# A four-step FFT filter and a low-rank token mixer on one core: last FFT stage and low-rank product in one matmul over 96 rows

## The chip, the cores and the metric

One core of one Trainium2 chip. The metric is the device time of the whole kernel in microseconds (us). Executions of one kernel mostly lie within about 1% of their median; now and then one falls into a slower state, in which the TensorE clock in the trace's records is lower throughout. Only fast executions are compared here. The core's own span in a profile is some 2 us shorter than the device time. In the profile lines PE stands for TensorE's matmuls, PEld for its weight loads, DVE for VectorE, ACT for ScalarE, POOL for GpSimd and SPq for SyncE's queue, which issues DMAs. The **pitch** of matmuls is the time from the start of one to the start of the next.

## The reference, cut to what matters

```python
X = np.fft.rfft(x, axis=1)                 # x: (8, 3136, 256)
y = np.fft.irfft(X * F, n=3136, axis=1)    # F: a complex filter per frequency and channel
h = y.T @ U @ V                            # along the sequence, rank 32
u = y + h.T
out = u + relu(u @ w_ch1) @ w_ch2          # 256 -> 1024 -> 256
```

The kernel writes 3136 as 64 x 49 and runs the FFT as matmuls: a first stage (`pf`, 64 points), a middle stage per frequency k1 (`pz` forward, multiply by the filter, `pe` back, 49 points), and a last stage (`pu`, 64 points back). The eight batches go through in five **units**: one batch each in units 0 and 1, two each in units 2, 3 and 4. While one unit's tokens go through the last stage and the two layers of the MLP (`phh`, `pc`), the next unit's first and middle stages are dealt in between.

## The kernel before: the parts that matter

The spectrum of a unit goes to DRAM (`ct2`) and is read back once, into tiles of 128 rows: 64 rows for one half of the residues r, 64 for the other. These tiles serve twice. The low-rank pass makes H = (U-hat)^T E from them:

```python
def low_rank(u):
    for rp in range(24):
        s, j, g = rp // 12, rp % 12, rp % 4
        nc.tensor.matmul(ph[32 * g:32 * g + 32, 0:bd],
                         ut2[:, rp * RANK:(rp + 1) * RANK],
                         u.e2[j // cj][:, s, j % cj, :], ...)
    ...                                            # one more for r = 48
    nc.scalar.copy(u.h1, ph[:, 0:bd])              # 4 partial sums of 32 rows
```

and the last stage reads them again, and adds H V by a second set of matmuls:

```python
def stage4(gr):                                    # a group is 512 tokens
    for dh in range(2):
        for i in range(4):                         # 8 matmuls of 128 columns in all
            nc.tensor.matmul(pu[:, dh, i * 128:(i + 1) * 128],
                             e2[:, y, j % cj + jj, d0:d0 + 128], s2, ...)
        for b in range(nb):                        # 4 of 256 columns in all
            nc.tensor.matmul(po[:, b], u.h1[:, d0:d0 + 128], vv[...], ...)
    nc.vector.tensor_copy(gr.ut, pu)
```

The plan deals the work in steps of about 1 us: the spectrum's loads 24 or 25 steps before a large unit's first group, the low-rank pass 6 steps before it. The order of each engine's instructions is fixed when the kernel is built.

## Time and profile before

| kernel before | |
|---|---|
| time, median | 634.8 us (632.4 to 640.6), 3 runs |
| span of the profiled run | 630.4 us |
| PE busy | 90% |
| bytes moved by DMA | 98.3 MB |

Two lines of the page, the granted clock in 40 slices of the span (9 is 90% of full speed or more) and the memory traffic:

```profile
PEclk9975569999999999999999999999999999999999
...
HBM read 59.88 MB, written 51.38 MB: 177 GB/s over the span
```

After the first unit's start every slice is at 9: the clock records are at full from 88 us to the last matmuls, and TensorE stands still for at most 3.2 us at a time. As **markers** I use the start of VectorE's cast to `ut` of each unit's first group: 81.5, 176.0, 259.2, 388.9 and 515.2 us in the kernel before. The two stretches in which the next unit's work is dealt most densely (columns: length; busy time and count of PE, PEld, DVE, ACT, POOL; clock; DMA share; GB/s):

```profile
81.50:176.00 94.50, 84.04 (x598) 56.63 (x597) 52.08 (x67) 50.59 (x102) 27.37 (x46) 0.96 0.94 222
176.00:259.20 83.20, 81.70 (x548) 51.80 (x547) 53.76 (x53) 49.82 (x91) 10.06 (x16) 1.00 0.72 187
```

The queue of SyncE at the end of unit 2's middle stage: the last spectrum store, output stores, and the first loads of that spectrum, which wait for the store to land.

```profile
227.31 0.32 SPq L360 DMA_DIRECT2D ct_2<-esb  x1
...
230.45 2.02 SPq L420 DMA_DIRECT2D e_2415<-ct_2  x2
```

3.1 us pass from the issue of the store to the loads. The pass's first matmul is at 248.4 in that trace, 18 us after the first load was issued; the pass's last tile, whose loads were issued from 236.9, was used at 256.2 after a wait of 0.2 us.

### The profile page before, as it was taken

To read this page: it belongs to the slowest core of one execution; us is meant where nothing else is said; L and a number is where in the kernel's file an instruction comes from. 1 tells how busy PE (TensorE), PEld (TensorE's weight loads), DVE (VectorE), ACT (ScalarE), POOL (GpSimd) and SP (SyncE) were. 2 spreads that over 40 slices of the span, in tenths; PEclk is the share of its full clock that TensorE was granted. 3 is DMA by queue.
4 is the path that set the end of the run, shared out by engine and by line. 5 is a ranking of instruction groups with operands and counts; after the bars stand their busy time and mean duration, and the time that the engine had idled before them with its cause. 6 is when DMAs were issued, how large, how long until landed. Compare 5 with 4: busy or idle time off the path is not lost.

```text
span 630.4 us, 10659 instructions
## 1 busy us (share of the span) xinstructions
PE 567.5 (90%) x4161; PEld 404.9 (64%) x4161; DVE 323.1 (51%) x376; ACT 332.1 (53%) x618; POOL 83.2 (13%) x136
## 2 busy tenths in 40 slices
PE   3178289799899999999999999999999999999995
PEld 0166146556556656667677677776777777777774
DVE  5165125676478853337777643476777223233231
ACT  0033046466366656464666665556565555555552
POOL 4230524314100113120001110100000000000000
PEclk9975569999999999999999999999999999999999
DMA  9797689999965579775437685826242753123033
GB/s 164 187 229 185 134 187 220 236 239 218 211 211 154 130 182 285 199 175 144 130 103 174 145 222 190 216 79 185 78 123 75 156 156 101 37 65 101 1 101 109
DMA packets 51993, 98.28 MB, mean 156 GB/s; under 512 B 7386, under 2 KB 29816, under 8 KB 51746
## 3 DMA queue, kind: packets, MB, share of 16 engines
q1 hardware_dynamic: 38742, 69.23, 40.0%
q0 software_dynamic: 11232, 27.20, 21.4%
q10 hardware_dynamic: 1968, 1.17, 0.7%
q8 instruction: 32, 0.52, 0.4%
q14 instruction: 19, 0.16, 0.1%
HBM read 59.88 MB, written 51.38 MB: 177 GB/s over the span
## 4 chain that ended last, share of the span: by engine, by line
PE 76%; DMA 18%; ACT 2%; SPq 1%; issue 1%; DVE 1%; POOL 0%; ACTq 0%; POOLq 0%
PE phh L497 24%; PE pc L541 23%; PE pe L347 8%; PE pz L379 5%; PE pu L482 3%; PE pu L488 3%; PE pc L513 3%; DMA ct_1<-esb 3%; DMA e_2424<-ct_2 3%; PE pf L285 2%; DMA a_342<-ct_0 2%; SPq L420 1%; DMA a_848<-ct_1 1%; DMA a_217<-ct_0 1%; DMA e_540<-ct_0 1%; DMA tf_77<-tf 1%
## 5 line engine op out<-in xcount | busy, mean ns | idle before, releaser
L497 PE MATMUL phh<-ut,w1sb 128*128 128x512 f16 (+2 forms) x848 | 245.8, 369 | 1.8 <-DVE ut L491 1.3
L394 DVE TENSOR_TENSOR uv<-pz,fab 98x1024 f16<-98x1024 f32 (+1 forms) x132 | 141.8, 1087 | 47.6 <-PE pz L379 46.1
L551 DVE COPY och<-pc 128x512 f32<-128x512 f32 x96 | 66.2, 690 | 148.4 <-PE pc L513 131.7
L358 ACT CAST esb<-pe 98x512 f16<-98x512 f32 (+1 forms) x160 | 79.9, 501 | 97.0 <-PE pe L347 78.4
L497 PEld LDWEIGHTS <-w1sb 128*128 128x128 f16 x848 | 105.9, 145 | 31.6 <-issue 8.9
L347 PE MATMUL pe<-uv,g_80 98*98 98x512 f16 (+1 forms) x330 | 90.3, 361 | 1.2 <-DMA g_80<-g 1.2
L491 DVE CAST ut<-pu 128x1024 f16<-128x1024 f32 x48 | 58.7, 1224 | 36.9 <-PE pu L488 36.0
L347 PEld LDWEIGHTS <-g_80 98*98 98x98 f16 x330 | 44.5, 138 | 18.3 <-issue 4.7
L513 PE MATMUL pc<-idn,ut 128*128 128x128 f16 x394 | 55.0, 219 | 0.0
L156 POOL DMA_DIRECT2D x<-in_x_dram x48 | 26.2, 558 | 181.4 <-PE pf L285 169.8
L379 PEld LDWEIGHTS <-tf_77 98*98 98x98 f16 x165 | 22.6, 137 | 32.8 <-issue 21.5
L513 PEld LDWEIGHTS <-ut 128*128 128x128 f16 x394 | 38.5, 98 | 6.8 <-issue 0.8
L290 DVE CAST asb<-pf 128x1024 f16<-128x1024 f32 x21 | 25.6, 1221 | 19.6 <-PE pf L285 18.8
L387 DVE TENSOR_TENSOR uv<-pz,fab 98x512 f16<-98x512 f32 x33 | 22.6, 691 | 12.5 <-PE pz L384 12.1
L285 PE MATMUL pf<-x,wf_64 128*128 128x512 f16 x84 | 25.7, 379 | 0.1
L288 ACT CAST asb<-pf 128x1024 f16<-128x1024 f32 x21 | 21.3, 1012 | 4.7 <-PE pf L285 4.2
L379 PE MATMUL pz<-a_168,tf_77 98*98 98x256 f16 x4 | 1.6, 406 | 14.7 <-DMA a_168<-ct_0 14.3
L433 PEld LDWEIGHTS <-ut_96 128*32 128x32 f16 x120 | 3.1, 101 | 16.0 <-DMA e_537<-ct_0 8.8
L305 POOL DMA_DIRECT2D ct_4<-asb x12 | 8.3, 700 | 36.2 <-ACT asb L288 36.2
L305 POOL DMA_DIRECT2D ct_2<-asb x12 | 8.5, 713 | 29.5 <-ACT esb L358 25.8
L358 ACT ACT_TABLE_LOAD x1 | 1.3, 1283 | 20.2 <-DMA ct_0<-asb 20.2
L285 PEld LDWEIGHTS <-wf_64 128*128 128x128 f16 x84 | 7.4, 98 | 4.3 <-issue 1.6
(1477 smaller groups left out, 1122.3 us busy)
## 6 DMA issues: line engine op xcount, KB each, us to landing
out_dram<-och SPq DMA_DIRECT2D x96, 192.0 KB
x<-in_x_dram POOLq DMA_DIRECT2D x48, 256.0 KB, 7.3
out_dram<-och SPq DMA_DIRECT2D x16, 384.0 KB
ct_2<-asb POOLq DMA_DIRECT2D x12, 256.0 KB, 6.5
ct_3<-asb POOLq DMA_DIRECT2D x12, 256.0 KB, 6.3
ct_4<-asb POOLq DMA_DIRECT2D x12, 256.0 KB, 5.6
ct_2<-esb SPq DMA_DIRECT2D x15, 196.0 KB
ct_3<-esb SPq DMA_DIRECT2D x15, 196.0 KB
```

Of the source, the lines that this page charges most:

```text
L156: nc.gpsimd.dma_start(t[64 * p:64 * p + 64], dram(x.tensor, (u.b[0] * SEQ + 8 * c) * DM + st * p, [[NR * DM, 64], [1, 8 * DM]]))
L285: nc.tensor.matmul(pf[:, i, :], wf1, u.x[c][:, r:r + 2, :], start=True, stop=True)
L290: nc.vector.tensor_copy(dst, pf)
L347: nc.tensor.matmul(pe[0:98, 0:bd], g3[:, (2 * k + l) * 98:(2 * k + l + 1) * 98], uv[:, l * bd:(l + 1) * bd], start=(k != 32 and l == 0), s ...
L358: nc.scalar.copy(st["esb"][:, i, :], pe[0:98, 0:bd])
L379: nc.tensor.matmul(pz[0:98, 0:bd], wz, a2[c][:, i, :], start=True, stop=True)
L394: nc.vector.tensor_mul(uv.rearrange("p (f b d) -> p f b d", f=2, b=nb), zin, fin)
L491: nc.vector.tensor_copy(gr.ut, pu)
L497: nc.tensor.matmul(ph[:, 0:n], w1v[:, dh, :, t], gr.ut[:, dh, 0:n], start=(dh == 0), stop=(dh == 1))
L513: nc.tensor.matmul(o[:, dh * 128:dh * 128 + 128], gr.ut[:, dh, t0:t0 + n], idn, start=False, stop=(dh == 1), skip_group_check=True)
L541: nc.tensor.matmul(o, gr.h[tt][:, i * 128:(i + 1) * 128], w2sb[:, tt * DM:(tt + 1) * DM], start=(tt == 0), stop=False, skip_group_check=True)
L551: nc.vector.tensor_copy(dst, gr.pc.rearrange("p (b j d) -> p b j d", b=u.nb, j=u.jc))
```

## The change

Intent: TensorE is the bound, so give it fewer columns. H is copied into rows 64 to 95 of the spectrum's own tile, and the moving operand is the table of the last stage over the matching columns of V. One matmul over 96 rows then does both products: 16 of 64 columns a group in place of 8 of 128 and 4 of 256. The price: the tiles hold 64 spectrum rows, so the low-rank pass, which wants 128, loads the spectrum a second time into a ring of three tiles of its own; H must be summed over its four partial sums and put on rows 64 to 95 by a matmul (`pk`); and H must be copied into every tile before the last stage can start. Apart from this the two real frequencies, k1 = 0 and 32, share one slot of the middle stage.

The diff, cut to its core:

```diff
-NK = 33
+NK = 32
 ...                                  # tables and filter rows for 32 slots
+    eb = [cst.tile([128, 8 * 512], F16, name=f"eb{i}") for i in range(3)]
+    def put_h(u, t, n):
+        nc.vector.tensor_copy(t[64:96, 0:n * bd]..., <u.h1 rows 64:96, repeated n times>)
+    def load_tiles():                 # as tiles come free
+            nc.sync.dma_start(t[0:64, 0:8 * bd], dram(u.ct2, 8 * c * bd, ...))
+            if u.h1 is not None and c < 3:
+                put_h(u, t, 8)
     def low_rank(u):
+        for c in range(3):
+            load(c)                   # ring of 3 tiles "eh", 128 rows
+        load_tiles()
+        yield
+        for c in range(nt):           # 3 pieces in a small unit, 6 in a large one
+            for i in range(nr): nc.tensor.matmul(ph[...], ut2[...], eh[c][:, i, :], ...)
+            if c + 3 < nt: load(c + 3)
+            if c + 1 < nt: yield
+        nc.scalar.copy(hp, ph[:, 0:bd])
+        nc.tensor.matmul(pk[0:96, 0:bd], kr, hp, start=True, stop=True)
+        nc.scalar.copy(u.h1[64:96, :], pk[64:96, 0:bd])
+        for c in sorted(u.e2): put_h(u, u.e2[c], 8)
+        put_h(u, u.e2l, 1)
     def stage4(gr):
+                nc.tensor.matmul(pu[:, dh, 64 * i:64 * i + 64], e2[0:96, d0:d0 + 128],
+                                 sv[0:96, 64 * r:64 * r + 64], ...)
-    deal(mids[2], 34, 44, S[2] - 25)  # loads at S - 24, the pass at S - 6
+    deal(mids[2], 33, 44, S[2] - 27)
+    deal_rank(units[2], S[2] - 26, S[2] - 7)   # loads at S - 26, bursts from S - 17 to S - 7
```

## The prediction

> **What bounds the kernel now.** I read the page first, then the table of stretches, then the timeline of TensorE in the steady part, at a boundary between two units (a unit is one or two batches) and round a low-rank pass.
>
> ```profile
> PE 567.5 (90%) x4161; PEld 404.9 (64%) x4161; DVE 323.1 (51%) x376; ACT 332.1 (53%) x618; POOL 83.2 (13%) x136
> PE 76%; DMA 18%; ACT 2%; SPq 1%; issue 1%; DVE 1%; POOL 0%; ACTq 0%; POOLq 0%
> ```
>
> The chain that ended last is 76% PE. The stretches (columns: length, then PE, PEld, DVE, ACT and POOL busy, granted clock, DMA share, GB/s) show where it is not:
>
> ```profile
> 30.00:66.00 36.00, 29.61 (x135) 23.85 (x133) 23.21 (x37) 12.16 (x34) 9.77 (x14) 0.65 0.85 192
> 82.80:178.00 95.20, 85.30 (x603) 57.32 (x603) 52.86 (x67) 51.17 (x103) 27.17 (x45) 0.97 0.93 224
> 260.00:414.00 154.00, 151.43 (x1140) 109.59 (x1138) 89.13 (x89) 94.61 (x168) 17.72 (x28) 1.00 0.63 164
> 414.00:520.00 106.00, 106.00 (x822) 77.42 (x820) 61.60 (x62) 64.06 (x119) 0.00 (x0) 1.00 0.48 127
> ```
>
> Up to 82.8 us the first unit waits on DMA. From 82.8 to 178 us DMA is 93% busy, and the chain runs partly through it. After 178 us PE is the bound. Busy PE overcounts, so I summed start-to-start pitches instead. The timeline has 0.216 us for 512 columns and 0.109 for 256; for 128 and 64 columns it shows:
>
> ```profile
> 404.57 0.60 PE L497 MATMUL phh<-ut,w1sb 128*128 128x512 f16 x2
> 405.01 0.39 PE L482 MATMUL pu<-s_78,e_4122 128*128 128x128 f16 x4
> 405.23 0.38 PE L488 MATMUL pu<-vsb,h_4428 128*128 128x256 f16 x2
> 405.45 0.39 PE L482 MATMUL pu<-s_78,e_4122 128*128 128x128 f16 x4
> 405.68 0.38 PE L488 MATMUL pu<-vsb,h_4428 128*128 128x256 f16 x2
> 405.89 0.27 PE L541 MATMUL pc<-w2sb,h_4512 128*128 128x256 f16 x1
> ...
> 280.16 0.19 PE L469 MATMUL pu<-s_78,e2l_97 128*128 128x64 f16 x1
> 280.19 0.19 PE L471 MATMUL pu<-vsb,h_2673 128*128 128x64 f16 x1
> 280.22 0.19 PE L469 MATMUL pu<-s_78,e2l_97 128*128 128x64 f16 x1
> ```
>
> Four matmuls of 128 columns take 0.22 us, 55 ns each; those of 64 take 29 ns each, every one behind a new stationary load of 128 columns. One group's last stage is 0.88 us (405.01 to 405.89). Summing pitches over all matmuls gives 523.6 us; of the elapsed time PE is short by 21 us in 82.8 to 178, by 8 in 178 to 260 and by only 7 after that. So PE time taken away after 178 us should come off the end, if no wait replaces it.
>
> **What the Trainium skill says.** "Perfetto Trace Analysis", introduction: matmul busy time misleads because matmuls are pipelined. The trace agrees: a 0.39 us span against a pitch of 55 ns. "TensorE: Matmul & The Clock Gate", Back-to-back issue gap: N/2.4 + 2.5 ns isolated, 81 ns sustained at N=128. The trace has 55 ns with loads, so the first form holds and the second does not. "TensorEngine Tiling (Array Packing)", Key Properties: changing the tiling mode drains TensorE. The low-rank pass uses 32-column tiles, and in this trace its edges cost some 0.1 us going in and 0.26 coming out. "VectorE: DVE Perf Modes", Side-by-side: a 16-bit copy inside SBUF can run four wide, 693 ns for 2048 elements; that would be (4096/4 + 150)/0.96 = 1.22 us for 4096. No instruction of the trace before shows such a copy; this figure is an estimate from the page.
>
> **The change part by part.**
>
> 1. Last stage. A group now has 16 matmuls of 64 columns over 96 rows: 16 x 29 ns = 0.46 us for 0.88. 48 groups x 0.42 = -20.2 us. The short groups lose half of 32 matmuls, -0.5 us.
>
> 2. Real pair in one slot. Each unit loses one z matmul and two pe matmuls: 3 x 0.216 for three large units, 3 x 0.109 for unit 1, about one slot (0.85 us in the timeline at 57 to 64 us) in unit 0: -3 us. DVE loses five multiplies of 0.69 to 1.22 us, beside PE.
>
> 3. Replication matmul `pk`: five of 0.11 to 0.22 us, +0.9 us. Pitches summed over the built order of the changed kernel give 501.3 us, -22.2 in all.
>
> 4. Low-rank pass in pieces. A burst of 25 in the trace before: the first at 385.37, the next ordinary matmul at 386.97. The built order now has six bursts of four with ordinary work between in the large units (in unit 2 the last two together). Each pair of mode edges costs about 0.37 us, so five more are +1.8 us per large unit: +5.4 us.
>
> 5. H under the spectrum. This is the new chain. Before, at the start of unit 2:
>
> ```profile
> 257.06 0.38 PE L437 MATMUL ph<-e2l_97,ut_96 128*32 128x512 f16 x1
> 257.47 0.59 ACT L440 CAST h_2673<-ph 128x512 f16<-128x512 f32 x1 [3.27 <-PE ph L437]
> 258.11 0.38 PE L482 MATMUL pu<-s_78,e_2415 128*128 128x128 f16 x4
> 259.19 1.23 DVE L491 CAST ut<-pu 128x1024 f16<-128x1024 f32 x1 [0.86 <-PE pu L488]
> 260.90 1.02 PE L497 MATMUL phh<-ut,w1sb 128*128 128x512 f16 x4
> ```
>
> From the last low-rank matmul (257.06) to the end of `ut` is 3.4 us, filled with the old group's second-layer matmuls. Now it is: matmul 0.4, cast 0.6, `pk` 0.4, cast 0.6, hand-overs 0.1 (2.1 so far), then the H copy into tile 0 (1.22), and on DVE, in the built order, the copies into tiles 1 and 2 and the small one (2.7) before `ut` (1.23): 7.3 us. What lies beside it is in the built order of PE. In units 2 and 4 nearly all of the old group's matmuls stand before the last low-rank burst; between it and the first `phh` are 0.9 and 1.2 us of work, so some 6 us idle in each. Unit 3 has 4.2 us of filler, 3 idle. Unit 1 has copies half as long (a chain of 5.0) and 1.2 of filler: 3.8, for 1.6 before, so +2.2. Then the first group of the new unit has no second-layer matmuls to fill in, and its 8 relus of 0.6 us outlast its 8 pairs of 0.43 plus the next stage: some +0.8 each in units 2 to 4. Sum: 6 + 3 + 6 + 2.2 + 2.4 = about +19 us.
>
> 6. Unit 0. Same loads in six pieces; the slot saved (-0.85), the H chain (+1.7 at copies of 0.7 us), no copies of V between partitions: about 0. The two POOL writes of the moving operand, at the trace's 2.4 ns an element (1818 ns for 768), take 7.4 us each, ahead of need.
>
> 7. Bytes. The spectrum is read twice, 12.8 MB more of 98. Where DMA is 93% busy that is 0.8 MB for unit 0's later tiles, 3.5 us at 224 GB/s; the output stores, now spread evenly, ease it. Of 2.5 us that PE saves there I count none. Unit 2's loads reach its low-rank pass just in time now (a wait of 0.23 us), and more bytes go ahead of them: 0 to +3.
>
> Sum: -22.2 + 5.4 + 19 = +2.2, less some 2 because two of the passes were split already in the trace before; parts 6 and 7 together I put at 0: about 0. So 635 us.
>
> **Rivals.** (A) The columns saved come off in full: the fillers cover the H chain, or the data arrive early. For it: PE is bound after 178 us, and the 29 ns pitch is measured. Against it: the static order puts the fillers first. It gives 635 - 20 + 5 = 617 to 620 us. (B) The H copies run one or two wide, 4.4 or 2.3 us each. Then each boundary grows by 9 or 3 us: 645 to 665 us. Against it: both sides are 16-bit and contiguous. (C) Doubled spectrum traffic delays units 1 and 2, in a stretch that is 93% DMA: +5 to +8 us there, 641 us. The share of 0.48 to 0.63 later speaks against it for units 3 and 4. (D) The 96-row form loads its weights more slowly than 128 rows: at 55 ns a pitch nothing would be saved, about 650 us.
>
> **Range and chances.** The saving (22 us) is sure to two or three; the boundary stalls (19) are worked out from durations and a static order and may be off by 8; DMA adds 4 either way. Together about +-10, with B and D as a tail above and A below: 621 to 649. Under 622 I give 0.13, over 647.5 it is 0.16, between them 0.71.
>
> **What would show it.** Right: sixteen `pu` at a pitch near 29 ns (0.46 us a group); after 260 us fewer busy PE microseconds and new gaps of 3 to 7 us at the starts of units 2, 3 and 4, put down to DVE (`ut` or the tile written with H); H copies of about 1.2 us. Wrong: a `pu` pitch over 40 ns (D), H copies of 2 us and more (B), no gaps at the boundaries and a time under 622 (A), or long PE waits for spectrum loads (C).

## The result, and the profile after

The changed kernel took 652.8 us (median of four runs: 704.3, 650.4, 650.9, 654.8), the kernel before 633.6 in the same session. The run of 704 us was in the slow state, and it was the profiled one, so I ran the kernel again for a clean profile (first experiment): 656.1 us. Ratios in this text are the mean time of one kernel's fast runs over that of the other's of the same rounds, so not quite the ratio of the medians. Ratio: **1.0307** (95%: 1.022 to 1.039), slower. The prediction had 635 us, from 621 to 649.

All that follows reads the profile of the repeated run, span 653.0 us. Page lines:

```profile
span 653.0 us, 11086 instructions
...
PEclk9986598999679997979999999899999997999999
...
HBM read 72.30 MB, written 51.38 MB: 189 GB/s over the span
...
PE 65%; DMA 6%; DVE 3%; ACT 2%; issue 1%; SPq 1%; POOL 0%; ACTq 0%; DVEq 0%
```

PE's share of the chain fell from 76% to 65%, memory reads rose by 12.4 MB as intended, and the clock line has seven slices below 9 after the first six, where the kernel before has none. The markers tell where the time went:

| marker (us) | unit 0 | unit 1 | unit 2 | unit 3 | unit 4 | end of span |
|---|---|---|---|---|---|---|
| before | 81.5 | 176.0 | 259.2 | 388.9 | 515.2 | 630.4 |
| after | 78.5 | 182.2 | 282.5 | 418.1 | 547.6 | 653.0 |
| difference | -3.0 | +6.2 | +23.3 | +29.2 | +32.4 | +22.6 |

So 23 us are lost by unit 2's first group. From there to the end the two kernels take the same: 371.2 us before, 370.5 after. The two early stretches (columns as before):

```profile
78.50:182.20 103.70, 82.87 (x623) 55.92 (x623) 50.14 (x66) 49.18 (x101) 27.71 (x46) 0.89 0.93 220
182.20:282.50 100.30, 85.07 (x595) 53.89 (x595) 58.94 (x59) 50.84 (x94) 10.06 (x16) 0.93 0.74 188
```

PE is busy for about as long as before in each, but over 9 and 17 us more, and at a clock of 0.89 and 0.93. What PE waits for, from 82 us on (line and tile, releaser, us in all, times, longest):

```profile
PE ph L462 <- DMA eh<-ct: 18.2, 4, 8.7
PE pf L300 <- DVE ut L518: 6.0, 2, 3.1
...
PE phh L527 <- DVE ut L518: 4.2, 2, 2.7
PE pu L515 <- DVE eb L417: 4.0, 3, 1.9
```

The first line is new: the low-rank pass stands 18 us waiting for its own loads, in units 1 and 2. The other three are the H chain (`eb` is the tile that H is copied into); together they are 14 us.

**The wait for loads.** SyncE's queue at the end of unit 2's middle stage, as shown above for the kernel before, and PE's wait:

```profile
238.42 0.31 SPq L364 DMA_DIRECT2D ct<-esb  x1
...
248.35 4.41 SPq L444 DMA_DIRECT2D eh<-ct  x6
```

```profile
255.69 0.62 PE L462 MATMUL ph<-eh,ut 128*32 128x512 f16 x4 [8.70 <-DMA eh<-ct]
```

The last spectrum store takes 9.9 us from its issue to the loads that wait for it (3.1 before), the loads need 7 more, and the plan has the first **burst** (a piece of the low-rank pass, four matmuls in a row) 9 steps after the loads where the kernel before had 18. At unit 1 it is the same: 9.7 us for 5.9 before, and PE waits 6.0, 1.8 and 1.6 us for the three pieces. "DMA: Bandwidth & Descriptors" of the Trainium skill, Anatomy of one DMA, fits a DMA from GpSimd with 2 us plus its bytes over 436 GB/s, some 2.5 us for a store of 196 KB (an estimate, for the store here goes out from SyncE); the traces have 3.1 us where the next unit's first x load was issued 2.6 us behind the store, at 229.95, and 9.9 where 1.5 MB of x loads, first-stage stores and output stores (256 KB each) were issued between 236.5 and 239.2, round the store.

**The H chain** at unit 2's start, on PE and on VectorE:

```profile
276.67 0.38 PE L469 MATMUL ph<-e2l,ut 128*32 128x512 f16 x1
277.72 0.38 PE L474 MATMUL pk<-hp,kr 128*96 128x512 f16 x1 [0.67 <-ACT hp L472]
280.01 0.64 PE L515 MATMUL pu<-sv,eb 96*128 96x64 f16 x16 [1.92 <-DVE eb L417]
283.74 1.01 PE L300 MATMUL pf<-x,wf 128*128 128x512 f16 x2 [3.08 <-DVE ut L518]
```

```profile
278.74 3.49 DVE L417 COPY eb<-h 32x4096 f16<-32x4096 f16 x3 [6.09 <-ACT h L476]
282.15 0.28 DVE L417 COPY e2l<-h 32x512 f16<-32x512 f16 x1
282.46 1.23 DVE L518 CAST ut<-pu 128x1024 f16<-128x1024 f32 x1
```

From the last low-rank matmul to the end of `ut` are 7.0 us (7.3 predicted), the three copies and the small one stand ahead of the cast, and PE's gaps, from the end of one matmul's pitch to the next matmul, are 0.8, 2.1 and 3.25 us.

**The clock.** The clock records of the trace show windows of 3.4 us, or two to five of them in a row, at 0.5 after most such stops: at 108.1 (3.4 us), 169.5 (17.1), 251.5 (10.2), 282.2 (6.8), 418.7 (3.4) and 545.0 (6.8), 47.7 us in all; the kernel before has none between 88 us and its last matmuls. One of them in the table of stretches:

```profile
252.00:256.00 4.00, 0.31 (x4) 0.11 (x4) 0.00 (x0) 0.00 (x0) 0.00 (x0) 0.50 1.03 271
```

In these windows PE did work worth 14.8 us at full speed, so it took PE 14.8 us more (not all of that need reach the end). "TensorE: Matmul & The Clock Gate", Part 1, describes this (half rate after an idle window of 3.4 us). The trace agrees on the rate and on the length of the windows; the stops that were enough can be shorter, 3.1 us at 416.2 and 2.1 us at 543.1. Length alone does not decide: this stop of the same trace, 3.4 us from the end of the last pitch, was followed by no such window, nor was one of 3.2 us in the kernel before (110.7 to 113.8).

```profile
116.75 0.38 PE L378 MATMUL pz<-a,tf 98*98 98x256 f16 x2 [3.24 <-DMA a<-ct]
```

In each trace all these windows start whole multiples of 3.41 us apart. That a stop costs when it fills enough of one interval of this grid fits the cases named here: the stops at 416.2 and 543.1 filled 2.4 and 1.9 us of one interval, the two without a window, which lie across a border, at most 1.8 and 1.7. No run tests it.

### The profile page after: what moved, and what is told of

The parts are those of the page before. It is cut to its first block, busy times and chain, and to the rows that moved or that the text cites. A ratio compares the mean times of both kernels' runs of the same rounds, so it can differ in the third digit from the quotient of the medians.

```text
span 702.5 us, 11086 instructions
## 1 busy us (share of the span) xinstructions
PE 619.0 (88%) x4350; PEld 414.7 (59%) x4350; DVE 333.8 (48%) x388; ACT 336.4 (48%) x623; POOL 88.6 (13%) x138
## 4 chain that ended last, share of the span: by engine, by line
PE 78%; DMA 14%; DVE 4%; ACT 1%; issue 1%; SPq 1%; POOL 0%; ACTq 0%; DVEq 0%; POOLq 0%
PE phh L527 27%; PE pc L570 25%; PE pe L356 9%; PE pz L378 5%; PE pc L542 3%; PE pu L515 3%; PE pf L300 3%; DMA ct_0<-asb 2%; DMA a_392<-ct_0 1%; DMA ct_1<-esb 1%; DMA a_227<-ct_0 1%; DMA ct_2<-esb 1%; PE ph L462 1%; DMA ct_1<-al 1%; SPq L444 1%
## 5 line engine op out<-in xcount | busy, mean ns | idle before, releaser
L527 PE MATMUL phh<-ut,w1sb 128*128 128x512 f16 (+2 forms) x848 | 278.6, 412 | 6.5 <-DVE ut L518 6.5
L393 DVE TENSOR_TENSOR uv<-pz,fab 98x1024 f16<-98x1024 f32 (+1 forms) x128 | 138.5, 1088 | 68.4 <-PE pz L378 67.0
L527 PEld LDWEIGHTS <-w1sb 128*128 128x128 f16 x848 | 111.1, 147 | 46.9 <-issue 16.3
L356 PE MATMUL pe<-uv,g_81 98*98 98x512 f16 (+1 forms) x320 | 96.2, 390 | 1.2 <-DMA g_81<-g 1.2
L518 DVE CAST ut<-pu 128x1024 f16<-128x1024 f32 (+2 forms) x53 | 60.6, 1143 | 39.0 <-PE pu L515 38.9
L542 PE MATMUL pc<-idn,ut 128*128 128x128 f16 x394 | 59.2, 234 | 0.0
L300 PE MATMUL pf<-x,wf_64 128*128 128x512 f16 x84 | 29.7, 438 | 9.4 <-DVE ut L518 5.7
L462 PE MATMUL ph<-eh,ut_97 128*32 128x512 f16 (+1 forms) x120 | 11.0, 403 | 22.9 <-DMA eh<-ct_0 10.8
L386 DVE TENSOR_TENSOR uv<-pz,fab 98x512 f16<-98x512 f32 x32 | 21.5, 689 | 10.2 <-PE pz L383 9.5
L515 PEld LDWEIGHTS <-eb_98 96*128 96x128 f16 x256 | 11.9, 107 | 13.1 <-DVE eb_98 L417 9.3
L515 PE MATMUL pu<-sv,eb_98 96*128 96x64 f16 x256 | 13.1, 207 | 5.1 <-DVE eb_98 L417 5.0
```

What stands on the lines that cost most here:

```text
L300: nc.tensor.matmul(pf[:, i, :], wf1, u.x[c][:, r:r + 2, :], start=True, stop=True)
L356: nc.tensor.matmul(pe[0:98, 0:bd], g3[:, (2 * k + l) * 98:(2 * k + l + 1) * 98], uv[:, l * bd:(l + 1) * bd], start=(l == 0), stop=(l == 1))
L393: nc.vector.tensor_mul(uv.rearrange("p (f b d) -> p f b d", f=2, b=nb), zin, fin)
L515: nc.tensor.matmul(pu[:, dh, 64 * i:64 * i + 64], e2[0:96, d0:d0 + 128], sv[0:96, 64 * r:64 * r + 64], start=(i == 0), stop=True, skip_gro ...
L518: nc.vector.tensor_copy(gr.ut[:, :, 0:n], pu[:, :, 0:n])
L527: nc.tensor.matmul(ph[:, 0:n], w1v[:, dh, :, t], gr.ut[:, dh, 0:n], start=(dh == 0), stop=(dh == 1))
```

## The experiments

Each table row below is one kernel's markers; they are read with the two rows above. Ratios are to the kernel before, in the same rounds.

| run | unit 0 | unit 1 | unit 2 | unit 3 | unit 4 | end | median us | ratio (95%) |
|---|---|---|---|---|---|---|---|---|
| e1_again | 78.5 | 182.2 | 282.5 | 418.1 | 547.6 | 653.0 | 656.1 | 1.0376 (1.0327 to 1.0426) |
| e2_warm | 74.6 | 179.3 | 275.5 | 408.6 | 539.1 | 643.3 | 645.9 | 1.0227 (1.0171 to 1.0282) |
| e3_put_pool | 75.9 | 186.8 | 279.3 | 416.8 | 545.1 | 651.2 | 654.0 | 1.0329 (1.0279 to 1.0380) |
| e4_half_reads | 79.2 | 181.0 | 272.2 | 402.1 | 525.1 | 631.4 | 633.8 | 0.9998 (0.9971 to 1.0025) |
| e5_pair_only | 79.5 | 176.1 | 258.8 | 387.5 | 512.9 | 627.5 | 628.4 | 0.9906 (0.9873 to 0.9940) |
| e6_pass_early | 74.4 | 180.8 | 282.4 | 414.8 | 540.5 | 646.6 | 647.2 | 1.0199 (1.0141 to 1.0256) |
| e7_share | 82.0 | 185.6 | 279.8 | 414.5 | 544.1 | 650.3 | 652.9 | 1.0265 (1.0180 to 1.0350) |
| e8_all_moves | 73.0 | 186.5 | 268.5 | 410.4 | 535.4 | 642.1 | 646.8 | 1.0193 (1.0135 to 1.0252) |
| e9_cut_reads | 78.1 | 179.8 | 279.2 | 414.4 | 544.8 | 650.7 | 654.1 | 1.0321 (1.0260 to 1.0383) |
| e10_hybrid | 78.7 | 170.5 | 256.9 | 398.9 | 527.1 | 633.6 | 635.0 | 0.9997 (0.9970 to 1.0023) |
| e11_x_late | 76.7 | 183.5 | 276.4 | 419.0 | 548.8 | 654.8 | 653.5 | 1.0305 (1.0241 to 1.0369) |
| e12_hybrid2 | 78.2 | 169.6 | 262.0 | 408.9 | 538.0 | 641.8 | 640.8 | 1.0098 (1.0068 to 1.0127) |
| e13_last_unit | 79.7 | 172.8 | 258.7 | 388.1 | 517.3 | 625.2 | 627.6 | 0.9875 (0.9831 to 0.9920) |

Markers come from one profiled run each; unit 0's differs by some 4 us between runs of like kernels. e1 to e4 ran together and e5 to e8 together, all on one chip; e9 and e10, e11 and e12, and e13 on three others. So ratios, not medians, are compared across calls.

My theories at the start: (1) the H chain's stops and the half clock after them; (2) spectrum loads late in units 0 to 2; (3) the splitting of the low-rank pass; (4) a slower 96-row matmul.

### e1_again: the changed kernel, unaltered

> The changed kernel unaltered, for a profile in the fast state (the profile taken with the result was in the slow one). Expected: 651 us (650 to 655), some 3% over the kernel before. Theory 1 (stalls of the H chain at the starts of units 1 to 4, and the half-clock windows that follow each of them): gaps of TensorE of about 2, 6, 3 and 5 us at the four starts, and after 178 us at least six windows of 3.4 us at clock 0.5, some 25 to 40 us at half clock in all. Theory 2 (spectrum loads late in units 0 to 2): 15 us or more of waits on DMA before 285 us. Theory 4 (the 96-row matmul is slower): pitch of the last stage over 40 ns; if it is near 29 ns, theory 4 is out.

Measured: 656.1 us. Gaps at the four starts 4.6 (in five parts), 6.2, 3.1 and 5.3 us; waits for loads of 18 us before 285 us; the pitch of the 96-row matmuls, start to start over 137 of them between 440 and 540 us, is 29.0 ns. Theory 4 is out. Theories 1 and 2 both have their marks.

### e2_warm: matmuls that nobody needs, in the gaps

```diff
+        if gr.g == 0 and u.n:          # before the first last-stage matmul of a unit
+            for _ in range(9 if u.nb == 2 else 5):
+                nc.tensor.matmul(pu[:, 0, 0:bd], u.hp[:, 0:128], u.hp, start=True, stop=True)
+        if gr.g == 0 and gr.u.n and t == 0:   # before the first matmul of the MLP
+            for _ in range(14 if gr.u.nb == 2 else 4):
+                nc.tensor.matmul(ph, e[0:96, 0:128], e[0:96, 0:512], start=True, stop=True)
```

> The changed kernel with matmuls that nobody needs put where TensorE stands still at a unit's start (9 of 64 rows and 512 columns into the last stage's PSUM tile before the first group of a large unit, 5 for unit 1; 14 and 4 before the first matmul of the first layer). The result is the same, and the chain of casts and H copies is as long. Theory 1: the half-clock windows after 260 us vanish and the time falls by about half of their length, 8 to 15 us, to 637 to 643 us; the boundaries still take as long as their chain. If the stalls alone count (no cost of the clock), the time stays at 651 or rises by 1 to 3 us where the fillers overshoot. Theory 2: no change, since the waits on loads before 178 us are left.

Measured: ratio 1.0227 for 1.0376, some 9 us faster with more work for TensorE. At unit 2's start:

```profile
271.00 2.10 PE L507 MATMUL pu<-hp 128*128 128x512 f16 x9
273.08 0.64 PE L520 MATMUL pu<-sv,eb 96*128 96x64 f16 x16
```

No half-clock window is left between 189 us and the last matmuls, and the work that ran in such windows fell from 14.8 to 9.2 us. So the clock's cost is real. Its size is less sure: from unit 2's marker to the end the profile gained 2.7 us, where the work in the windows that vanished there had been 6.4, so the needless matmuls take some of it back; the rest came before that marker, by a shorter start-up (3.9 us, which nothing in the edit explains) and a shorter wait for loads at unit 2.

### e3_put_pool: all H copies but the first on GpSimd

```diff
-            put_h(u, u.e2[c], 8)
+            put_h(u, u.e2[c], 8, nc.vector if c == 0 else nc.gpsimd)
```

> The changed kernel with only tile 0's H copy on VectorE at a unit's start; the copies into tiles 1 and 2 and the small one go to GpSimd. Takes 2.7 us off the chain ahead of the first cast to ut of units 2, 3 and 4 and 1.4 off that of unit 1[...]. Theory 1: gaps at the starts fall by 2 to 3 us each, fewer half-clock windows follow, time 651 - 9 (chain) - 4 to 8 (clock) = 634 to 639 us. Theory 2 (loads): no more than 2 us. If GpSimd slows VectorE, the copies and casts grow past 1.3 us and the gain is below 5 us.

Measured: ratio 1.0329, 3 us at most, less than expected. The gap before the MLP at unit 4's start fell from 2.9 to 1.5 us, as it should. But GpSimd takes some three times as long for a copy as VectorE (1.2 us):

```profile
543.12 8.12 POOL L417 COPY eb<-h 32x4096 f16<-32x4096 f16 x2 [119.95 <-ACT h L476]
```

GpSimd also issues the next unit's x loads, which queue behind these copies, and the stretch to unit 1's marker grew from 103.7 to 110.9 us. And copies on the two engines took longer where they met. At unit 3's start VectorE's copy began 0.4 us after one on GpSimd (411.05 to 414.64) and ended 1.1 us after it, 4.27 us for 1.22:

```profile
411.45 4.27 DVE L417 COPY eb<-h 32x4096 f16<-32x4096 f16 x1
```

Where GpSimd's copy began just after VectorE's, it took 4.6 us for 3.6. So the expectation's last sentence came true at this start. Inconclusive on the sizes.

### e4_half_reads: the pass uses its first three pieces twice

```diff
             if c + 3 < nt:
-                load(c + 3)
+                eh[c + 3] = eh[c]
```

> The changed kernel where the low-rank pass loads only its first three pieces and uses them twice: the result is wrong on purpose (H from half of the spectrum), everything else is the same. 4.7 MB fewer reads, and the built order of the large units is another: all low-rank bursts come early, then the old group's second-layer matmuls stand between the cast of H and the first matmul that needs it. Theory 1: stalls at the starts of units 2 to 4 below 1 us each and no half-clock windows after 260 us; 651 - 15 (stalls) - 8 to 15 (clock) = 621 to 628 us, so faster than the kernel before. Theory 2 (bytes alone): most of the gain before 285 us, 651 - 5 to 10 = 641 to 646, with the stalls of units 3 and 4 left. Theory 3 (the splitting of the pass costs): no more than 5 us.

Measured: wrong on purpose, 633.8 us, ratio 0.9998: all of the loss is gone, but nothing is gained either. With no reload, the built order has all low-rank bursts early and the old group's matmuls behind `pk`: there is no gap over 0.7 us at the starts of units 2 to 4 and no half-clock window from 259 us to the last matmuls. From unit 2's marker to the end it takes 359.2 us (371.2 before): here the saved columns come off undisturbed. The wait for the first loads of unit 2's pass is still 9 us, and unit 1's marker as late as in e1. The 621 to 628 us of theory 1 were missed by what is lost ahead of unit 2. The edit takes 4.7 MB of reads away as well as changing the order, so it does not tell the two apart at the later starts; e6, which changes the order alone, does for units 3 and 4. What is left ahead of unit 2 is mostly the wait for loads (17.7 us in the two passes).

### e5_pair_only: the kernel before with only the real pair in one slot

```diff
-NK = 33
+NK = 32        # and its tables, filter rows, row order of the last stage's table
```

> The kernel before with only the real pair k1 = 0, 32 in one slot (32 slots, the filter rows and the rows of the last stage's table in the new order). One z matmul and two pe matmuls fewer per unit, one slot of 33 in the DMA-bound first unit. My prediction's step 2: -3 us, 634 to 631. If the saved columns come off where TensorE is the bound and not elsewhere, -2 to -3; if unit 0 or the filter loads (more small DMAs) suffer, 0 or slower.

Measured: ratio 0.9906, 4 to 8 us faster; the profile has 2.9 us. Part 2 of the prediction was right in sign and not too large; this part alone beats the kernel before.

### e6_pass_early: the pass of units 3 and 4 stands 12 steps earlier

```diff
-        deal(mids[u.n], 33, ..., S[u.n] - 28)
-        deal_rank(u, S[u.n] - 27, S[u.n] - 7)
+        deal(mids[u.n], 33, ..., S[u.n] - 40)
+        deal_rank(u, S[u.n] - 39, S[u.n] - 19)
```

> The changed kernel with only the plan of units 3 and 4 altered: the slots of the middle stage end 12 steps earlier and the low-rank pass stands 12 steps (some 12 us) earlier. The built order then has some 50 and 40 of the old group's matmuls between the replication matmul and the first that needs H. Theory 1 (H chain uncovered): the gaps of TensorE at the starts of units 3 and 4 (3.1 us and 5 us in the fast profile, and some 2 us of half clock after them) vanish; 656 - 9 to 12 = 644 to 647 us; units 1 and 2 stay as they are. If instead the stalls come from VectorE or DMA itself, the gaps move to another place and the time stays within 2 us.

Measured: ratio 1.0199, 11 us faster than e1. Unit 4's start on PE, as shown above for the changed kernel:

```profile
534.41 0.38 PE L469 MATMUL ph<-e2l,ut 128*32 128x512 f16 x1
...
535.46 0.38 PE L474 MATMUL pk<-hp,kr 128*96 128x512 f16 x1
...
538.04 0.64 PE L515 MATMUL pu<-sv,eb 96*128 96x64 f16 x16 [0.24 <-DVE eb L417]
```

Between the three PE has other work, the wait for the H copy is 0.24 us for 1.9, and there is no half-clock window from 289 us to the last matmuls. From unit 3's marker to the end: 231.8 us, for 241.5 before and 234.9 in e1. From unit 2's marker on it is 6.3 us shorter than e1, all that the two profiles differ by. The H chain of units 3 and 4 cost where the order left it bare.

### e7_share: units 0 and 1 use the pass's tiles in the last stage too

```diff
-    pending = [(u, c) for u in units for c in range(6)]
+    pending = [(u, c) for u in units for c in range(3 if u.nb == 1 else 0, 6)]
+        if u.nb == 1:                    # H goes over the upper half, after the pass has read it
+            for c in range(3): u.e2[c] = eh[c]
```

> The changed kernel where units 0 and 1 (one batch each) use the low-rank pass's own tiles for the last stage's first three chunks, with H written over the upper half once the pass has read it: 1.6 MB fewer reads, 0.8 MB of them between the last spectrum store of unit 1 and its first group. Correct result. VectorE gets six H copies of 0.7 us at the start of units 0 and 1 in place of three, so +2 us of chain at each. Theory 2 (the second read of the spectrum queues on DMA that is over 90% busy): from the first group of unit 0 to that of unit 1 3 to 7 us shorter by the reads (103.7 us in the last profile), less the 2 of the copies; time 656 to 650. Theory 1: no gain, or 2 to 4 us slower for the copies.

Measured: ratio 1.0265, some 7 us faster than e1 by the means (the intervals overlap), but not where I expected it: the stretch to unit 1's marker is unchanged (103.6), and the one to unit 2's is 6 us shorter (94.2). In this run a wait of 7.1 us for the middle stage's loads appeared at 109 us. That fewer reads help is not shown by this run.

### e8_all_moves: what the runs so far pointed to, together

```diff
 # e7_share, and e6_pass_early with the pass of unit 2 10 steps earlier too
-        for c in sorted(u.e2): put_h(u, u.e2[c], 8)
+        put_h(u, u.e2[0], 8)             # the others one chunk ahead of their use
-        deal_f1(u, S[u.n - 1] - (38 if u.n == 3 else 48), (1, 7))
+        deal_f1(u, S[2] - 12, (1, 3, 5, 7))      # unit 3
```

> All that the runs so far point to, with a correct result: tiles shared in units 0 and 1; of the H copies only that into the first tile at a unit's start, the others one chunk ahead of their use; the middle stage and the low-rank pass of unit 2 10 steps and of units 3 and 4 12 steps earlier; unit 3's first stage, whose x loads fell on unit 2's spectrum store and loads, 26 steps later. If theories 1 and 2 together tell the whole: gaps at the unit starts below 2 us each, no wait of over 3 us for spectrum loads after 178 us: 656 - 11 (units 3, 4) - 8 to 14 (unit 2) - 5 to 8 (unit 1) = 623 to 632 us, faster than the kernel before (634). If something else holds the kernel (the 96-row form, the split pass), it stays over 640.

Measured: 646.8 us, ratio 1.0193; it fell short by 15 us. The stretch from unit 1 to unit 2 came down to 82.0 us as wished. But the middle stage of unit 2, moved earlier, fell into the stretch ahead of unit 1 in which DMA is full: 113.5 us (103.7), with a wait of 7.3 us for its loads; and unit 3's middle stage then waited 6.4 us for its first stage. The waits moved; they did not go.

### e9_cut_reads: fewer bytes for units 0 and 1, the same order

```diff
+            m = 1 if u.n == 1 or (u.n == 0 and c > 2) else 8
-            nc.sync.dma_start(t[0:64, 0:8 * bd], ...)
+            nc.sync.dma_start(t[0:64, 0:m * bd], ...)
```

> The changed kernel where the last stage's tiles of unit 0 from the fourth chunk on and of unit 1 altogether are loaded with one of their eight columns of blocks only (wrong result on purpose, same order of work): 0.69 MB fewer reads for unit 0, 0.69 MB fewer for unit 1's first three tiles, both between the first group of unit 0 and that of unit 1, and 0.69 MB fewer after it. Theory 2 (that stretch lasts as long as its bytes take at 220 GB/s): 1.38 MB are 6 us, so the stretch falls from 103.7 to 97 to 98 us, and the next one by 0 to 3; time 656 to 647 to 650. If the reads are hidden and the stretch is long for another reason (the H chain of unit 1, the order of work): within 2 us of 656.

Measured: wrong on purpose, ratio 1.0321, 3 us faster than e1 and within the error of no change; the stretch ahead of unit 1 is 101.7 us (103.7). Theory 2 in the form "the stretch lasts as long as its bytes" is refuted. The reads that I cut stand behind the pass's loads in the queue, or long ahead of them; the last store still took 9.5 us to land.

### e10_hybrid: the merged last stage in units 3 and 4 only

```diff
 # e5_pair_only, and
+        self.merged = n >= 3             # tiles of four residues, H copied two groups ahead
+        # units 0 to 2: tiles of 128 rows read once, H from pk added by a second matmul
+        # units 3, 4: the pass on its own loads, S - 39, bursts from S - 29 to S - 19
```

> A version made of what the runs show, with a correct result: the real pair in one slot; units 0, 1 and 2 with the last stage of the kernel before (tiles read once, 128 rows, H added by a second matmul), units 3 and 4 with the merged last stage, their low-rank pass 12 steps earlier on loads of its own, H copied into each tile two groups ahead. The extra reads fall where DMA has room and the columns are saved where TensorE is the bound. Theories 1 and 2: up to the first group of unit 2 as with the real pair alone (259 us); from there to unit 3 and to unit 4 128 and 125 us, then 92 and 15: 619 us; half a microsecond for each burst's mode edges and 1 us of replication at each start may cost 3 more: 618 to 624 us, 1.5 to 2.5% below the kernel before and below the 628 of the real pair alone. If merging itself costs something that these theories leave out, it will be at 628 or above.

Measured: 635.0 us, ratio 0.9997. Up to unit 2's marker it was as hoped (256.9 us). Then unit 3's marker came 142 us later in place of 128: the last store of unit 3 was issued at 345 and its loads at 354.9, PE waited 5.2 us for them and ran 6.8 us at half clock. The DMA share was 0.8 to 1.0 from 345 to 360, with the next unit's x loads, its first-stage stores and output stores.

### e11_x_late: unit 3's first stage later

```diff
-        deal_f1(u, S[u.n - 1] - (38 if u.n == 3 else 48), (1, 7))
+        deal_f1(u, S[2] - 14, (1, 3, 5, 7))      # unit 3
```

> The changed kernel where unit 3's first stage, and with it its x loads, is dealt 24 steps later (in twice as many slots of each group); nothing else. In the fast profile of the changed kernel unit 2's last spectrum store was issued at 238.4 and landed at 248.3, with 1 MB of unit 3's x and first-stage stores issued between 236.5 and 240; the pass's loads came after it and TensorE stood still for 8.9 us. If that collision makes the wait (theory 2 as mended: not the bytes in all, but what stands in the queues when the last store goes out, and a plan that leaves 9 steps between the loads and the first burst where the kernel before left 19): the store lands in 4 to 6 us, the wait falls to 2 to 5 us, and the stretch from the first group of unit 1 to that of unit 2 falls from 100.3 to 93 to 96 us; the next stretch may lose 0 to 4 to a first stage that ends later; time 656 to 649 to 654. If the wait has another cause, it stays at 8 to 9 us.

Measured: the last store's loads went out after 4.4 us for 9.9:

```profile
239.99 0.31 SPq L364 DMA_DIRECT2D ct<-esb  x1
...
244.38 3.77 SPq L444 DMA_DIRECT2D eh<-ct  x6
```

The wait of 8.7 us before the pass was gone (no wait at its first burst, 0.5 and 2.8 us inside it), and the stretch from unit 1 to unit 2 fell to 92.9 us (100.3), as expected. The next stretch gave it back: 142.6 us for 135.6, with 4.3 us of wait for unit 3's own first stage. Ratio 1.0305. So what was issued round the last store made most of that wait; and that traffic has to go somewhere.

### e12_hybrid2: the hybrid with the pass 16 steps behind its loads

```diff
-            plan[step_at(S[u.n] - 19 - 2 * (5 - i))].append(rk)
+            plan[step_at(S[u.n] - 13 - 2 * (5 - i))].append(rk)
-    rank_step = {step_at(S[u.n] - 6): ...}
+    rank_step = {step_at(S[u.n] - 7): ...}
```

> The hybrid of the last call (merged last stage in units 3 and 4 only, real pair in one slot) with two numbers of the plan changed: the first burst of the low-rank pass stands 16 steps after its loads were issued in place of 10 (in the hybrid's profile unit 3's last store took 9 us to land, the loads 6.5 more, and TensorE stood still for 5.2 us and ran 6.8 us at half clock after it), and the pass of units 1 and 2 one step earlier. If the late loads are what cost the hybrid its gain: no wait for these loads above 1 us, the stretch from unit 2 to unit 3 falls from 142 to 130 to 133 us, and the time from 635 to 623 to 627 us. If not, it stays at 633 or more.

Measured: 640.8 us, ratio 1.0098, slower than the first hybrid. My expectation was wrong:

```profile
381.20 0.61 PE L465 MATMUL ph<-eh,ut 128*32 128x512 f16 x2 [6.47 <-DMA eh<-ct]
```

The loads went out at 360.4 and the first bursts, at 368.5, did not wait; but the pass's second ring of loads stood in the queue behind six tiles for the last stage and output stores, with the DMA share at 0.8 to 1.0 from 350 to 385 us. Ten us of half clock followed. The edit changes two things, and the other hurt as well: with the pass of unit 2 one step earlier PE waited 3.1 us for its loads at 244.6 and ran 6.8 us at half clock, and 6.0 us were lost between the markers of units 1 and 2 against e10, 4.9 between those of units 2 and 3. More slack for the first loads did not help here, where the later loads were held up in their turn.

### e13_last_unit: the merged last stage in unit 4 only

```diff
-        self.merged = n >= 3
+        self.merged = n == 4
```

> The hybrid with the merged last stage in unit 4 alone; units 0 to 3 keep the last stage of the kernel before (their spectrum is read once). Correct result. In the 25 us before unit 4's first group the DMA engines have nothing to do for a next unit: their share there was 0.14 to 0.6 in the 20 us ahead of the loads, where before unit 3 it was 0.8 to 1.0. If doubled reads cost because they fall into stretches in which DMA is full (units 1 to 3), and the merged matmuls are worth what their pitches say where they do not: no wait for loads of the pass in unit 4, from the first group of unit 4 to the end 107 us for 115 of the kernel before, from unit 3 to unit 4 125 to 128, and up to unit 3 what the real pair alone gave (387.5 us) plus 0 to 4 for the replication of H in units 0 to 3: 619 to 625 us, 1.5 to 2.5% below the kernel before. If merging has a cost of its own, it stays at 628 (the real pair alone) or above.

Measured: correct, 627.6 us, ratio **0.9875** (0.983 to 0.992): faster than the kernel before, and not separable from e5 (0.9906). It missed the 619 to 625 us that I expected. Ahead of unit 4 there is no next unit to load for. All that PE waited for after 480 us:

```profile
PE pc L644 <- DVE och L666: 0.3, 1, 0.3
```

From unit 3's marker to the end: 237.1 us; the kernel before has 241.5, the real pair alone 240.0. So merging is worth 2.9 us in this unit, by one profile of each kernel: 6.7 us won after unit 4's marker (107.9 for 114.6) and 3.8 lost before it (129.2 for 125.4), where the pass in pieces stands. The pieces sum to about that: 12 groups of 0.42 us are 5.0 saved, and ten bursts in place of two cost 2.3 more in changes of tile mode (2.9 us for 0.6), leaving 2.7.

## Why the prediction was wrong, point by point

**The columns, parts 1 to 3: right.** The pitch is 29.0 ns. Summing pitches by columns over the trace gives 501.2 us for 523.6 before: -22.4, predicted -22.2. The real pair gave 3 to 6 us, predicted 3.

**The split pass, part 4: high by half.** A burst of four, which run side by side in four tiles of 32 columns, takes 0.425 us of PE's time, 0.21 more than one matmul of 512 columns; the 0.37 for each pair of edges is too much; it comes out if the pass's last matmul, which runs alone, is counted at a quarter of its pitch. Six bursts cost 1.4 us beyond their pitches, where the kernel before spent 0.4 in unit 3 (one burst) and 0.6 in unit 4 (two): +1.0 and +0.8 a unit for +1.8. For all three units the prediction had 3.4 net of the passes that were split already.

**The H chain, part 5: right.** Predicted idle of about 4, 6, 3 and 6 us at the starts of units 1 to 4; measured 4.6, 6.2, 3.1 and 5.3 (the 4.6 is 3.8 if the matmuls between, which ran at half clock, are given twice their pitch). A copy of 4096 elements took 1.22 us, as estimated (rival B is out). e6 shows that it is the bare order that costs.

**The bytes, part 7: the step that failed.** I wrote "Unit 2's loads reach its low-rank pass just in time now (a wait of 0.23 us), and more bytes go ahead of them: 0 to +3", and set it at 0 in the sum. The pass's loads cost 18.2 us of waiting in units 1 and 2. For the large units I had gone by DMA shares over stretches of 106 and 154 us (0.48 and 0.63); in the 20 us in which a spectrum is read back the share is 0.85 to 1.06, in the kernel before too (230 to 250 and 365 to 385 us). And I had not compared the slack: 18 steps from the loads to the pass before, 9 in the new plan. My own number was the sign: with 18 steps the last tile came just in time. Rival C had this mechanism at 5 to 8 us, less than half of what came, and I gave it little weight. What is shown, for unit 2: the wait falls from 8.7 us to 3.3 when the next unit's traffic around the store goes (e11), and it stays when only later bytes are cut (e9). In unit 4, where the queues have room, PE did not wait for a second read (e13). The slack of 9 steps was not tested alone in the changed kernel. What is not settled is how the 4 us by which unit 1's last store lands later divide between the bytes and the order in which they were issued.

**The clock: a term that I left out.** The prediction has no line for it. Work worth 14.8 us ran at half speed after the stops, so each stop cost more than its length. In e2, where TensorE is kept busy through the stops, the time is down though the chain is as long as before; 2.7 us of that lie after unit 2's marker.

The sum as it should have been: -22 columns, +1 x 3 for the split, +17 for the H chain (the gaps, 19.2, less some 2 at the same places before), +18 for the loads, +15 for the clock: +31. Measured +22.6. The parts overlap (a stop of one kind shortens the next, and unit 1 and 2 reach their waits earlier by the columns saved), so I call this an account and not a proof of each share.

After unit 2's marker the predicted sum came out, in part by luck: -15.5 for columns, -1.3 for the pair, +3.6 for the split and +11.4 for the H chains of units 3 and 4 and the relus are about -2, and -0.7 was measured; but 6.4 us of half-clock work lie there too, for which the sum has no line, so other terms were too high by some 5 us (the split by 1.8 in units 3 and 4; the rest is not placed). The miss in the total lies ahead of that marker.

## What to carry to other kernels

Columns taken from the engine that bounds a kernel come off the end only if no chain is laid bare and no queue fills: ask of every added load what stands ahead of it at that moment, in a window of its own length, and not what the DMA share is on average. Price an idle gap of 2 to 3 us on TensorE with a half-clock window that may follow it (2.1 us was enough once, 3.4 us was not another time), and look at the built order to see which work is left to cover a new chain. Then apply a change only where its price is low: of the correct kernels with a merged stage only the one that merges the last unit alone, where nothing else was being loaded, came out under the kernel before, and its gain over the real pair alone is not clear of noise. The price is that of a place in the plan, and not of the change: from unit 2's marker to the end e6, merged throughout, took 364.2 us, the kernel before 371.2 and the real pair alone 368.7 (one profile each); what e6 lost, it lost ahead of that marker.

## What the Trainium skill lacked or had wrong

- "TensorE: Matmul & The Clock Gate", Part 1, says that for modelling the warm-up penalty is under 1% of a typical span. That is said of the ramp; stops in the middle of a kernel, which the same part describes for another kernel, are not in it: here the half rate cost PE 14.8 us of 653, 2.3%, with TensorE 85% busy. The page's rule for kernels is no gaps over some 3 us; here the clock fell 1.9 us into a stop of 2.1 us at unit 4's start (545.0), which followed 120 us without a stop over 0.4 us, and did not fall for stops of 3.2 us (kernel before, 110.7) and 3.4 us (113.4).
- "DMA: Bandwidth & Descriptors", Anatomy of one DMA, gives a fit of a fixed cost plus bytes for one DMA, with no term for other traffic. The last spectrum store of a unit, under 200 KB, took 3.1 us to land in one trace and 9.9 in another, where 1.5 MB had been issued round it within 3 us, and at most 4.4 when the next unit's x loads and first-stage stores were moved away (e11).
- "TensorEngine Tiling (Array Packing)", Key Properties, says that a change of mode drains TensorE and gives no cost. Here going in and out for a burst of four matmuls in 32-column tiles cost 0.21 us, in the four traces with such bursts in which it was summed (e1, e2, e6, e13).
- "TensorE: Matmul & The Clock Gate", Back-to-back issue gap, says that at small sizes the isolated form under-counts a stream of loads and matmuls, with 81 ns for 128 columns. Here such a stream ran at the isolated form: 55 ns for 128 columns in the kernel before, and 29.0 ns for 64 columns behind a new stationary load (64/2.4 + 2.5 = 29.2).
